# Transposing the convolution's weights among the set-up work, with the matmul fills and the written order renumbered

## The chip, the cores and the metric

The kernel runs on one core of one Trainium2 chip. Its time is the device time of one execution, in microseconds (us); the number given for a kernel is the median of several runs. The profile is of one execution of its own, which has its own time.

Engines are named as in the profile: PE is TensorE (matmuls and transposes), PEld its weight loads, DVE is VectorE, ACT is ScalarE, POOL is GpSimd and SP is SyncE, which here only issues DMAs. Each works through its own queue in order and waits on semaphores for the others.

## What is computed

Linear attention without softmax, a root-mean-square norm over each head, then a feed-forward block with a convolution of three taps along the sequence as its gate. Batch 8, 8 heads, sequence 576, head size 64, model width 512, hidden width 1024:

```python
kv = np.einsum('bhsd,bhse->bhde', k, v)
out = np.einsum('bhsd,bhde->bhse', q, kv)
rms = np.sqrt(np.mean(out * out, axis=-1, keepdims=True) + 1e-06)
x = out / rms * g_norm                      # then heads are joined: [8, 576, 512]
h = np.maximum(x @ w_in, 0.0)
hp = np.concatenate([zeros, h, zeros], axis=1)          # one row on each side
conv_out = sum(conv_w[k][None, None, :] * hp[:, k:k + S, :] for k in range(3))
gate = 1.0 / (1.0 + np.exp(-conv_out))
out = (h * gate) @ w_out
```

conv_w has the shape 3 x 1024: three taps for each hidden channel.

## The kernel before

**Groups.** The 8 batches are worked in five groups: batch 0, batch 1, then 2 and 3, 4 and 5, 6 and 7. For each group the attention is computed with its result transposed (channels on partitions), then `h` in blocks of 128 channels, then the convolution and the gate, then the product with `w_out`, 128 rows at a time, stored to HBM.

**Attention of batch 0.** It comes in two parts, of six and two heads, so that work can begin when six heads have landed. `kv_mm` makes k^T v into `kv_ps`; `kv_out` copies that to `kv_sb`. For each pair of heads `tr_mm` transposes q into `qT_ps`, `tr_out` copies it to `qT`; `out_mm` multiplies qT and kv into `ot_ps`. From `ot_ps`, `square` (on ACT) makes the squares for the norm and `keep` copies the product, scaled by `g_sb`, to `o32`. `ss_mm` sums the squares over each head with the matrix `sel`, `ln_exp` (ACT) makes 1/rms of it, `rb_mm` spreads that over the partitions with the matrix `spread32`, into `rb_ps`, and `x_mul` (DVE) multiplies it to `o32`, which gives `xT`.

**The convolution.** For batch 0 it runs on PE, with diagonal matrices `diag` (one 128 x 128 for each tap and block) as weights, into `c_ps`. The other groups convolve on DVE and ACT: a `tap` is h times a weight for each partition, taken from `cw_rel`, and `add` adds it at its shift. `cw_rel` holds the outer taps divided by the middle one, and the middle one itself, which the sigmoid on ACT applies as its scale.

**The weights of the convolution.** `cw_rows`, 24 x 128 in float32, is loaded by SP as it lies in HBM. A transpose on PE (`cw_mm`) puts the channels on partitions, in `cw_ps`; `cw_out` (DVE) copies it to `cw`. Then `cw_ratio`, eight small DVE operations, makes `cw_rel`, and `cw_diag`, called three times, multiplies the identity by each tap, for `diag`, 128 x 1024 each time.

**Set-up.** Ahead of the groups stand: 14 warm-up matmuls on a tile of ones (`warm`), the loads of k, v and q, the loads of `g_sb` (two, on SP) and of `cw_rows` behind them, the matrix `sel`, 16 transposes of it on PE (`spread_ps`), the copy `spread`, 22 more warm-up matmuls, and `spread32`. This part is put in order by a scheduler from the source; in the built program all 36 warm-up matmuls come first on PE and the 16 transposes behind them.

**The order of the rest.** All that follows is recorded in a plan: each step is an entry with a number, an engine, an estimated cost and what it depends on. The text `ORDER` gives the sequence in which the entries are issued, and so the order in each engine's queue. A letter behind a number picks the engine where there is a choice (a: ACT, d: DVE), and `*n` puts n fills ahead of a PE step: matmuls of `ones` by `ones` into the PSUM buffer that the step then overwrites (`fill`), which compute nothing that is used. An entry on `LAND` issues nothing: it stands for data that have landed at the time given, for whoever makes the order. `Hold` says which steps hold a buffer, for the same purpose.

**Buffers.** PSUM has three buffers of two banks (`ps_two`: `ot_ps`, `rb_ps`, `h_ps`, `c_ps`) and two of one bank (`ps_one`: `warm_ps`, `spread_ps`, `cw_ps`, `kv_ps`, `qT_ps`, `ss_ps`, `o_ps`). Whoever takes a buffer waits until it has been read.

Of the kernel before, what the change touches and what calls it, by code (L numbers as in the profile page):

```python
# [25 lines left out]
def _patch_pnc_remap() -> None:  # L26
# [28 lines left out]
FP32 = mybir.dt.float32  # L55
# [18 lines left out]
PARTS = (3, 1)  # L74
NORM_TABLES = "natural_log_exp_and_others"
ORDER = """
    103 8 11 0 7 17*7 18d 9 19*6 20a 24 21*2 29 25d 26 104 22 30d 27 31*4 32 12 10 34*1 35d 36*1 23a
    37d 33d 41*1 42 38*1 1 43*2 40d 105 13 39 49*2 50 28d 44 2 47*2 106*4 48 6 107a 108 53*2 45*2 54
    3 114*1 109*1 110a 115a 51*1 124 125a 46 119 120a 52 55 64 56a 4 5 65d 111 112 116 117 126 127
    113d 118d 205 212 217 68 128a 121 14 122 66 213d 218a 204 69d 123d 129 130 59 60d 222 82 131 67  # L80
    86 83a 87d 203 70 71 72 57 58 84 85 132 133 223a 134 135 209 210a 138 136 137 208 227 61 139
    228d 62 63 88 89 90 140 141a 148a 235 236d 144 145a 150a 206 146 240 147d 151d 142 143d 149d
    241a 211 214 216a 207 215 367 152 153 154d 157d 155d 156d 158 170 15 164 171a 165a 229 231a 219
    230 232 233a 234 168 169a 73 74d 172d 250 251d 77 78d 75 221a 245 16 159 220 175a 374 79 76 80
    246d 375d 174d 378 379d 81 160 166 167d 242 243 247 249a 248 365 366 94 252 224 173d 244d 176
    177 179d 181d 180d 178d 95a 237 238 225 253 100 101a 226d 382 383d 368 255 256 369 182 96 257 91
    371*1 372d 239a 254a 184 373 258*4 259 185 92a 272*2 273 268*2 269 264*2 265 262*1 263 186 370
    390*1 391a 162 93 260*1 266*1 161 183 386*1 267 270 271 261 97 98a 376 384 377 187 274 393 276
    387a 385 388 389 163 200 394a 288 275d 277d 290d 278 280 279d 289d 281d 201a 392 405 406d 401
    291d 402a 282 523 283a 284 285a 292d 525 532 533d 403 404 524 407 408 397 398d 286 544 545d 380  # L90
    526 527 287a 293d 294 295 296d 299d 298d 297d 300 528 399 400 381 529 530a 531 395 306 320 396
    409 410 411 316 307a 317a 548 549a 202 102 550 321a 412 413 414 415 308 309a 322d 314 315a 324d
    301 318 319d 325d 310 536 311a 551 552d 537d 312 313d 326 559 560a 323d 555*1 556d 327 330d 331d
    328d 329d 538 534 539 332 546 535 540 553 554 541a 561 547 562 194 563 564a 195a 196 99 542 543
    557 558 565 566 188 189a 418 416 567 568 417 336 304 335 424 419 569 425 302 197 303 420 421 190
    422 423 191 192a 193 430 431 428 429 432 433d 444 445a 570 426 427 440 334 305 434 435a 448d
    441a 436 437d 333 337 438 439a 449d 198a 199 446 447a 451d 442 443a 450a 452 453 454d 466 464
    465a 470 467a 471a 457d 455d 359 360a 456a 458 480d 476 477a 478 472 473a 479a 468 571 572 573
    361 469a 481d 483d 474 475a 484 575 482d 485 486d 362 350 462 363a 351a 364 352 459 353 354a 355
    576 577 578 586 579 489a 460 344 345a 461 487d 488d 490 574 590 584 587 591 341 342a 493 347  # L100
    348a 349 346 585 494 492 343 338 580 588 581 582 583 356 589 491 592 593a 598 599a 596 597a 463
    339a 340 600d 622 623a 603d 495 594 595a 604 601a 602d 605 608d 606d 607d 609d 610 646 618 620
    647a 621a 616 617a 624d 627d 619a 628 644 626d 645a 357a 625d 629 631d 630d 632d 613 633d 634
    611 640 358 641a 642 502 643a 614 503a 504 612 648d 650d 649d 615 652 651d 653 654d 656d 655d
    657d 658 520 666 521a 635 522 505 637 506a 507 667a 499 500a 501 517 678 664 638 636 639 665a
    518a 519 668d 669d 687 670 671 659 673d 508 679a 509a 660 672d 510 511 512d 513 661 674 514 662
    702 663 515a 516 680d 676 703a 681 704 682 683d 684 675 677 688a 690 689d 691 692d 696 693 697a
    685 698 699 686 700a 705 701 706d 707 694 695 496 497d 498 708 709a 710 711 717 712a 713 714
    718a 719 715a 716 720 721a 722
"""  # L110
NF = 4
GROUPS = ((0,), (1,), (2, 3), (4, 5), (6, 7))
# [82 lines left out]
def kernel(  # L195
# [11 lines left out]
    nc = tc.nc  # L207
# [3 lines left out]
    P = 128  # L211
# [5 lines left out]
    n_ff = D_ff // P  # L217
# [4 lines left out]
    consts = pool("consts", 1)  # L222
# [8 lines left out]
    ps_one = pool("ps_one", 2, space=PSUM)  # L231
# [8 lines left out]
    def warm(n):  # L240
        for _ in range(n):
            nc.tensor.matmul(warm_ps, ones[:, :P], ones, start=True, stop=True)  # L242
# [34 lines left out]
    def load_w_out(half):  # L277
        fs = slice(half * n_ff // 2, (half + 1) * n_ff // 2)
        nc.gpsimd.dma_start(
            out=w_out_sb[:, fs, :], in_=moe_w_out.rearrange("(f p) m -> p f m", p=P)[:, fs, :])  # L280

    g_sb = consts.tile([P, 1], FP32, name="g_sb")
    for i in range(2):
        nc.sync.dma_start(out=g_sb[i * D:(i + 1) * D, :], in_=g_norm.unsqueeze(1))
    cw_rows = consts.tile([3 * n_ff, P], FP32, name="cw_rows")
    nc.sync.dma_start(out=cw_rows, in_=moe_conv_w.rearrange("k (f p) -> (k f) p", p=P))
    ident32 = consts.tile([3 * n_ff, 3 * n_ff], FP32, name="ident32")
    nc.vector.tensor_copy(ident32, ident[:3 * n_ff, :3 * n_ff])
    eps_sb = consts.tile([P, 1], FP32, name="eps_sb")
# [14 lines left out]
            nc.tensor.transpose(spread_ps[t * SM:(t + 1) * SM, c, :], sel[:, c, :], ident)  # L304
    spread = consts.tile([P, 4, P], BF16, name="spread")
    nc.vector.tensor_copy(spread, spread_ps)
    warm(22)

    spread32 = consts.tile([P, 2, P], FP32, name="spread32")
# [10 lines left out]
    plan = Plan()  # L320
# [3 lines left out]
    def ring(name, bufs):  # L324
        return rings.setdefault(name, Ring(bufs))


    TWO, ONE = ring("two", 3), ring("one", 2)
# [4 lines left out]
    def one_bank(shape, dtype, name):  # L333
        return ps_one.tile(shape, dtype, name=name, tag="one")
# [615 lines left out]
            g.o_ops.append(om)  # L950


    cw = consts.tile([P, 3, n_ff], FP32, name="cw")
    cw_rel = consts.tile([P, 3, n_ff], FP32, name="cw_rel")
    cst = {}

    def cw_mm():
        cst["ps"] = one_bank([P, 3 * n_ff], FP32, "cw_ps")
        nc.tensor.transpose(cst["ps"], cw_rows, ident32)

    def cw_out():
        nc.vector.tensor_copy(cw.rearrange("p k f -> p (k f)"), cst["ps"])

    def cw_diag(j):

        nc.vector.tensor_mul(
            diag[:, j, :, :], ident.unsqueeze(1).to_broadcast([P, n_ff, P]),
            cw[:, j, :].unsqueeze(2).to_broadcast([P, n_ff, P]))
# [10 lines left out]
        for j in (0, 2):  # L979
            nc.vector.tensor_mul(cw_rel[:, j, :], cw[:, j, :], sgn[:, 1, :])  # L980

    landed = plan.op("LAND", 9.0, None)
    mm = plan.op("PE", 0.3, cw_mm, deps=[landed])
    cw_done = plan.op("DVE", 0.2, cw_out, deps=[mm])
    Hold(ONE, mm, [cw_done])
    diag_done = []
    if any(map(any, C_PE)):
        diag = consts.tile([P, 3, n_ff, P], BF16, name="diag")
# [22 lines left out]
    for g in groups:  # L1011
        g.by_act, g.by_dma, g.x_from, g.kv_from = (c[g.n] for c in (BY_ACT, Q_DMA, X_FROM, KV_FROM))
        for b in g.bs:
            for name, src in (("k", k), ("v", v), ("q", q)):
                if b > 0:
                    need = []
                    if b > 1:
# [4 lines left out]
                        deps=[load_ops[name, b - 1]] if b > 1 else [])  # L1022
# [54 lines left out]
```

## Time and profile before

| | |
|---|---|
| median of 4 runs | 200.41 us (200.1 to 200.71) |
| time of the profiled execution | 200.71 us |
| its span, first to last instruction | 198.9 us |
| PE busy | 189.5 us, 95% of the span |
| DVE busy | 153.1 us, 77% |
| ACT busy | 139.0 us, 70% |
| DMA, mean over the span | 158 GB/s |
| diag product on DVE (L966) | 3 of 1.22 us |
| cw transpose on PE (L959) | 1 of 0.24 us, at 16.95 us |
| load of cw_rows (L286), issue | 0.60 us, at 2.00 us |

The time of a run is 1.8 us above the span: what lies around the instructions. The columns of the lines below are, in the chain of waits: start, length, engine, tile, line, how many; in the timeline: start, length, engine, line, operation, what is written and read with sizes, how many, and in brackets the idle time before and what ended it. An "x" after a shape counts instructions. In a list of one line's instructions the three durations are the least, the middle and the most in ns; in the list of waits the three numbers are the time in total, how many waits, and the longest.

How the time passes: up to 8.7 us PE runs warm-up matmuls while k, v and q come in; then batch 0 goes through attention with short steps that hand over between PE, ACT and DVE; from some 30 us on several groups overlap, and near the end there are only products with `w_out` and their stores.

### The profile page before, as it was taken

What the parts mean: (1) busy time and instruction counts of PE and PEld (TensorE: products, weight loads), DVE (VectorE), ACT (ScalarE), POOL (GpSimd) and SP (SyncE); (2) the same over time, 40 slices, a digit from 0 to 9 for tenths busy, and PEclk for the clock granted to TensorE, in tenths of its full rate; (3) what the DMA queues carried; (4) which work ended last, traced back from release to release, by engine and by line L of the source; (5) the groups of instructions that cost most, each with busy time, mean ns of one, the idle gap of its engine ahead of it and who ended that gap; (6) DMA issues with size and microseconds to landing.
All of it is one profiled execution on the core that took longest, in us unless ns stands there. A gap on an engine that the chain in (4) does not pass through costs nothing.

```text
span 198.9 us, 4714 instructions
## 1 busy us (share of the span) xinstructions
PE 189.5 (95%) x1910; PEld 118.5 (60%) x1910; DVE 153.1 (77%) x281; ACT 139.0 (70%) x211; POOL 40.5 (20%) x61
## 2 busy tenths in 40 slices
PE   7999998999999999999999999999999999999990
PEld 4675665887764555777854477654458754644440
DVE  2137678796989876769999999999989999988200
ACT  2036268878869986288897998787988788677131
POOL 7706030012414115011000699110000000000000
PEclk9999999999999999999999999999999999999999
DMA  4999999997899999997779721399551034354653
GB/s 48 199 203 203 205 207 205 203 206 119 124 189 204 226 208 225 203 176 103 182 183 230 228 54 53 94 248 233 146 160 54 0 112 119 86 149 131 164 150 98
DMA packets 32714, 31.49 MB, mean 158 GB/s; under 512 B 2332, under 2 KB 28084, under 8 KB 32692
## 3 DMA queue, kind: packets, MB, share of 16 engines
q0 software_dynamic: 20976, 16.25, 53.5%
q1 hardware_dynamic: 11716, 14.93, 29.0%
q8 instruction: 15, 0.25, 0.5%
q14 instruction: 7, 0.06, 0.1%
HBM read 37.24 MB, written 9.73 MB: 236 GB/s over the span
## 4 chain that ended last, share of the span: by engine, by line
PE 74%; DMA 9%; DVE 8%; ACT 5%; issue 1%; POOL 0%; DVEq 0%; ACTq 0%
PE o_ps L737 27%; PE h_ps L785 24%; DMA v_sb<-in_v_dram 6%; PE warm_ps L242 4%; PE ot_ps L371 3%; DMA kv_sb<-kv_sb 3%; PE qT_ps L460 3%; PE kv_ps L397 2%; PE c_ps L825 2%; PE rb_ps L660 2%; PE o_ps L928 2%; DVE tap L853 2%; ACT qT L349 2%; DVE h L884 2%; DVE conv L875 1%; DVE conv L873 1%
## 5 line engine op out<-in xcount | busy, mean ns | idle before, releaser
L785 PE MATMUL h_ps<-xT,w_in_sb 128*128 128x288 bf16 x512 | 67.4, 286 | 0.4 <-DVE h L798 0.3
L737 PE MATMUL o_ps<-w_out_sb,h 128*128 128x512 bf16 x272 | 61.4, 379 | 0.0
L785 PEld LDWEIGHTS <-w_in_sb 128*128 128x128 bf16 x512 | 48.6, 98 | 15.0 <-issue 2.2
L737 PEld LDWEIGHTS <-h 128*128 128x128 bf16 x272 | 25.7, 98 | 30.6 <-issue 1.4
L879 ACT ACTIVATE conv<-conv,cw_rel 128x576 bf16<-128x576 bf16 (+1 forms) x40 | 37.1, 962 | 1.7 <-DVE conv L875 1.6
L796 ACT ACTIVATE h<-h_ps 128x576 bf16<-128x576 f32 x46 | 28.9, 648 | 8.4 <-PE h_ps L785 8.2
L853 DVE TENSOR_SCALAR tap<-h,cw_rel 128x576 bf16<-128x576 bf16 (+1 forms) x73 | 29.7, 448 | 2.4 <-ACT h L796 1.3
L349 ACT ACTIVATE o_sb<-o_ps 128x512 f32<-128x512 f32 x33 | 19.7, 596 | 15.5 <-PE o_ps L737 10.9
L483 ACT ACTIVATE sq<-ot_ps 128x576 bf16<-128x576 f32 x32 | 19.6, 655 | 4.1 <-PE ot_ps L371 3.7
L884 DVE TENSOR_TENSOR h<-h,conv 128x1152 bf16<-128x1152 bf16 (+3 forms) x16 | 22.0, 1380 | 0.6 <-ACT conv L834 0.5
L864 POOL COPY conv<-h 128x4 bf16<-128x4 bf16 (+3 forms) x12 | 3.9, 324 | 89.4 <-ACT h L796 31.6
L875 DVE TENSOR_TENSOR conv<-conv,tap 128x1152 bf16<-128x1152 bf16 (+11 forms) x36 | 20.4, 621 | 1.1
L873 DVE TENSOR_TENSOR conv<-h,tap 128x1152 bf16<-128x1152 bf16 (+11 forms) x36 | 20.3, 620 | 0.9 <-ACT tap L851 0.4
L349 ACT ACTIVATE qT<-qT_ps 128x576 bf16<-128x576 bf16 x14 | 8.8, 649 | 16.6 <-PE qT_ps L460 16.6
L798 DVE TENSOR_SCALAR h<-h_ps 128x576 bf16<-128x576 f32 x18 | 13.3, 752 | 5.4 <-PE o_ps L928 2.7
L371 PE MATMUL ot_ps<-qT,kv_sb 64*64 64x288 bf16 x192 | 12.2, 297 | 1.9 <-ACT qT L349 0.6
L254 POOL DMA_DIRECT2D q_sb<-in_q_dram x9 | 6.8, 752 | 31.1 <-PE qT_ps L460 26.3
L678 DVE TENSOR_TENSOR xT<-o,rb_ps 128x576 bf16<-128x576 f32 x15 | 10.6, 750 | 3.3 <-PE rb_ps L663 1.6
L684 DVE SCALAR_TENSOR_TENSOR xT<-ot_ps,g_sb,rb 128x576 bf16<-128x576 f32 x16 | 12.2, 810 | 1.1 <-PE ot_ps L371 0.8
L460 PE MATMUL qT_ps<-ident,q_sb 96*128 96x96 bf16 x192 | 12.6, 206 | 0.1
L460 PEld LDWEIGHTS <-q_sb 96*128 96x128 bf16 x192 | 10.5, 97 | 2.5 <-issue 0.8
L371 PEld LDWEIGHTS <-kv_sb 64*64 64x64 bf16 x192 | 5.0, 104 | 9.3 <-issue 7.6
(76 smaller groups left out, 173.9 us busy)
## 6 DMA issues: line engine op xcount, KB each, us to landing
out_dram<-o_sb SPq DMA_DIRECT2D x24, 192.0 KB, 2.3
rb<-scr SPq DMA_DIRECT2D x16, 288.0 KB, 5.7
k_sb<-in_k_dram POOLq DMA_DIRECT2D x7, 576.0 KB, 11.5
v_sb<-in_v_dram POOLq DMA_DIRECT2D x7, 576.0 KB, 13.8
q_sb<-in_q_dram POOLq DMA_DIRECT2D x7, 576.0 KB, 12.0
out_dram<-o_sb SPq DMA_DIRECT2D x24, 128.0 KB, 2.4
out_dram<-o_sb SPq DMA_DIRECT2D x24, 64.0 KB, 2.0
w_in_sb<-in_moe_w_in_dram POOLq DMA_DIRECT2D x2, 512.0 KB, 15.1
```

The costliest lines, as they stand in the source:

```text
L349: nc.scalar.activation(dst, src, AX.Copy, scale=1.0 if scale is None else scale)
L371: nc.tensor.matmul(ps[i * D:(i + 1) * D, e, :HS], kv, g.qT[bi][es, 2 * t + i, :], start=True, stop=True)
L460: nc.tensor.transpose(ps[:, i, j * PS:(j + 1) * PS], q_sb[:, 2 * t + i, j * P:(j + 1) * P], ident[:PS, :PS])
L483: nc.scalar.activation(g.sq[bi, t], ust["ps"][:, :, :HS], AX.Square)
L737: nc.tensor.matmul(st["ps"][:n, :], g.h[:, f, t0:t0 + n], w_out_sb[:, f, :], start=(f == 0), stop=(f == n_ff - 1))
L785: nc.tensor.matmul(ps[:, e, :HS], w_in_sb[:, t, f * P:(f + 1) * P], g.xT[:, t, at:at + HS], start=(t == 0), stop=(t == n_hd - 1))
L796: nc.scalar.activation(dst, st["ps"][:, :, :HS], AX.Relu)
L853: nc.vector.tensor_scalar_mul(dst, src, cw_rel[:, j, f:f + 1])
L873: nc.vector.tensor_add(c[:, :, here], h[:, :, here], t[:, :, there])
L875: nc.vector.tensor_add(c[:, :, there], c[:, :, there], t[:, :, here])
L879: nc.scalar.activation(cst["c"][:, f - f0, :], cst["c"][:, f - f0, :], AX.Sigmoid, scale=cw_rel[:, 1, f:f + 1])
L884: nc.vector.tensor_mul(hs, hs, cst["c"])
```

## The change

Four things are edited.

1. `cw`, `cw_ps`, the transpose and the copy move from the plan into the set-up, behind the copy `spread` and ahead of the 22 later warm-up matmuls in the source. `cw_mm` and `cw_out` are gone as entries of the plan.
2. In their place one entry on `LAND` says that `cw` is there at 6.2 us. Before, an entry said that `cw_rows` is there at 9.0.
3. The load of `cw_rows` is issued on SP ahead of the two of `g_sb`.
4. `ORDER` is a new text. As the plan has two entries fewer, the numbers from 3 on are lower by 2. Once that is taken out, the sequence is the same but for these: `cw_ratio` and the three `cw_diag` stand at its very front (entries 4, 1, 2, 3), where before they stood between the steps of batch 0's norm, and fills are 50 instead of 57.

The fills that are dropped, one at each place, by the new numbers: the first kv product (15, 7 to 6), the third product of batch 0 (29, 4 to 3), an rb (43, 2 to 1; before at 23.53 us), a kv product (369, at 66 us), an rb (262, 2 to 1), a kv product (384, at 70.65 us) and a transpose of q (553, at 100.27 us).

```diff
 ORDER = """
-    103 8 11 0 7 17*7 18d 9 19*6 20a 24 21*2 29 25d 26 104 22 30d 27 31*4 32 12 10 34*1 35d 36*1 23a
-    37d 33d 41*1 42 38*1 1 43*2 40d 105 13 39 49*2 50 28d 44 2 47*2 106*4 48 6 107a 108 53*2 45*2 54
-    3 114*1 109*1 110a 115a 51*1 124 125a 46 119 120a 52 55 64 56a 4 5 65d 111 112 116 117 126 127
...
+    0 4 1 2 3 101 6 9 5 15*6 16d 7 17*6 18a 22 19*2 27 23d 24 102 20 28d 25 29*3 30 10 8 32*1 33d
+    34*1 21a 35d 31d 39*1 40 36*1 41*2 38d 103 11 37 47*2 48 26d 42 45*2 104*4 46 105a 106 51*2 43*1
+    52 112*1 107*1 108a 113a 49*1 122 123a 44 117 118a 50 53 62 54a 63d 109 110 114 115 124 125 111d
...
 """
...
+    cw_rows = consts.tile([3 * n_ff, P], FP32, name="cw_rows")
+    nc.sync.dma_start(out=cw_rows, in_=moe_conv_w.rearrange("k (f p) -> (k f) p", p=P))
     g_sb = consts.tile([P, 1], FP32, name="g_sb")
     for i in range(2):
         nc.sync.dma_start(out=g_sb[i * D:(i + 1) * D, :], in_=g_norm.unsqueeze(1))
-    cw_rows = consts.tile([3 * n_ff, P], FP32, name="cw_rows")
-    nc.sync.dma_start(out=cw_rows, in_=moe_conv_w.rearrange("k (f p) -> (k f) p", p=P))
...
     spread = consts.tile([P, 4, P], BF16, name="spread")
     nc.vector.tensor_copy(spread, spread_ps)
+
+    cw = consts.tile([P, 3, n_ff], FP32, name="cw")
+    cw_rel = consts.tile([P, 3, n_ff], FP32, name="cw_rel")
+    cw_ps = ps_one.tile([P, 3 * n_ff], FP32, name="cw_ps", tag="one")
+    nc.tensor.transpose(cw_ps, cw_rows, ident32)
+    nc.vector.tensor_copy(cw.rearrange("p k f -> p (k f)"), cw_ps)
     warm(22)
...
-    cw = consts.tile([P, 3, n_ff], FP32, name="cw")
-    cw_rel = consts.tile([P, 3, n_ff], FP32, name="cw_rel")
-    cst = {}
-
-    def cw_mm():
-        cst["ps"] = one_bank([P, 3 * n_ff], FP32, "cw_ps")
-        nc.tensor.transpose(cst["ps"], cw_rows, ident32)
-
-    def cw_out():
-        nc.vector.tensor_copy(cw.rearrange("p k f -> p (k f)"), cst["ps"])
...
-    landed = plan.op("LAND", 9.0, None)
-    mm = plan.op("PE", 0.3, cw_mm, deps=[landed])
-    cw_done = plan.op("DVE", 0.2, cw_out, deps=[mm])
-    Hold(ONE, mm, [cw_done])
+    cw_done = plan.op("LAND", 6.2, None)
     diag_done = []
```

## The prediction

> **What bounds the kernel now.** I read first the shares by engine, then the chain of work that ended last, then the timeline of VectorE (DVE) between 9 and 30 us, where the change acts, and last the waits.
>
> ```profile
> PE 189.5 (95%) x1910; PEld 118.5 (60%) x1910; DVE 153.1 (77%) x281; ACT 139.0 (70%) x211; POOL 40.5 (20%) x61
> ```
>
> TensorE (PE) is busy for 189.5 of 198.9 us. Of its 9.4 idle us 1.23 lie before its first matmul and 4.87 after 180 us, so some 3.3 us are spread over everything between: a delay of PE at the start has little to be absorbed in. The chain of waits (start, length, engine, tile, line) around the first attention group:
>
> ```profile
> 8.70 0.34 PE spread_ps L304 x16
> 9.03 0.96 PE kv_ps L359 x7
> 10.00 1.26 PE kv_ps L397 x72
> 11.26 0.84 PE qT_ps L359 x6
> ...
> 12.39 0.66 ACT qT L349
> 13.05 0.04 issue
> 13.09 0.32 PE ot_ps L371 x4
> ...
> 16.42 0.82 DVE o L353
> 17.24 0.04 issue
> 17.28 0.41 PE rb_ps L359 x2
> ```
>
> The reader is to see that the first product of q and kv starts at 13.09, released by ScalarE's (ACT) copy of qT, and that from 17.28 PE runs on almost without a gap. The other operand of that product, kv_sb, is copied by DVE, and it was early:
>
> ```profile
> 9.09 0.42 DVE L306 COPY spread<-spread_ps 128x512 bf16<-128x512 bf16 x1 [4.40 <-PE spread_ps L304]
> 9.55 0.48 DVE L316 SCALAR_TENSOR_TENSOR spread<-spread,neg 128x256 f32<-128x256 bf16 x1
> 11.30 0.56 DVE L351 CAST kv_sb<-kv_ps 128x384 bf16<-128x384 f32 x1 [1.27 <-PE kv_ps L397]
> ...
> 19.63 0.17 DVE L962 COPY cw<-cw_ps 128x24 f32<-128x24 f32 x1
> ...
> 21.77 0.17 DVE L973 TENSOR_SCALAR sgn<-cw 128x8 f32<-128x8 f32 x1
> ...
> 23.02 0.24 DVE L980 TENSOR_TENSOR cw_rel<-cw,sgn 128x8 f32<-128x8 f32 x2
> ...
> 27.19 2.35 DVE L966 TENSOR_TENSOR diag<-ident,cw 128x1024 bf16<-128x1024 bf16 x2
> ```
>
> kv_sb was done at 11.86, so 13.05 - 11.86 = 1.19 us of slack lay between it and the product. The weights' work sat at 19.6 to 29.5, in holes of DVE.
>
> **The change, part by part.** *The place that the weights' work gets.* By the order of the built program, PE still runs all 36 warm-up matmuls (L242) before the 16 spread transposes, although the source has 14 before and 22 behind; the new cw transpose comes after the spread transposes, as row 17, not between the warm-ups. And on DVE the order is: copy of spread, copy of cw, spread32, the eight small operations of cw_ratio, three diag products, and only then the copy of kv_sb. DVE takes its queue in order, so what is added there is ahead of kv_sb.
>
> *DVE, step by step.* The spread copy starts at 9.09 as before and ends at 9.51. The cw transpose (0.24 in its row, L959) runs from about 9.04 to 9.28 and is ready before that. Copy of cw: 0.17 plus a gap of 0.04, 9.72. spread32: 0.48, 10.23. cw_ratio from its first to its last operation took 21.77 to 23.26, 1.49: 11.75. diag: two took 2.35, so a second one starts 1.13 after a first that takes 1.22, and three take 1.22 + 2 x 1.13 = 3.48: 15.25. Copy of kv_sb 0.56: about 15.8 instead of 11.86, 3.9 late. That is 5.2 us of work put into an idle time of 1.27.
>
> *PE until then.* The fill of the first kv now waits for DVE, since cw_ps has taken the buffer of warm_ps and kv_ps must take one that DVE empties: 9.55 (spread copied) to 9.72 (cw copied) instead of 9.03, with six fills for seven (0.96 - 0.84 = 0.12 each). The kv product ends at 11.7 instead of 11.26, still 3.5 before DVE comes to it, so this 0.4 is hidden by the new wait; without that it would be on the path. Then six fills and the first qT transposes, 0.84 + 0.27, to 12.8; ACT copies it to 13.45; the second qT (in the built program it waits for ACT) and two fills, to 14.0; then PE stands until kv_sb at 15.8.
>
> *From kv_sb on.* First product at 15.83 instead of 13.09, 2.74 late: 3.9 less the slack of 1.19. Behind it in PE's queue stand the third qT, the next products and the second part of kv; on ACT the squares, all shifted. The third product was held before by four fills (0.60, to 14.61); now it comes after three, when DVE has copied the third qT. DVE: second qT 15.7 to 16.2 (0.46), third qT 16.55 (its transposes end at 16.35, with drain) to 17.0; product at 17.06. So 17.06 - 14.61 = 2.45 late. What follows is the same row of work to the copy of o (16.42 before) and the first rb at 17.28, which becomes 19.73. The squares on ACT, three of 0.65 from 16.2, end at 18.15, before the copy of o at 18.87, so they don't add.
>
> *What comes back.* From 17.28 to 29.9 the chain holds PE and ACT pieces alone, back to back (rb, ss, kv, qT, h): DVE's xT waits there for rb, not the other way. Taking 5.2 us off DVE there gives the chain nothing; the diag of 27.19 ends at 29.54, 0.1 before h needs DVE. The cw transpose at 16.95 lay beside the copy of o and gives 0; so does the copy of cw. One fill fewer before the rb of 23.53 is on the chain: -0.12. Of four later fills three stand at 66 to 71, before a load that lands at 71.31, the fourth at 100.27 beside ACT's copies; I take 0, bounds -0.5 and 0.
>
> *Queues.* On SP the load of cw_rows goes ahead of the two of g_sb. One issue took 0.60 and g_sb's landing 2.3, so cw_rows lands near 4, wanted at 9.04; g_sb some 0.6 later, wanted after 18. Cost 0; if cw_rows were later than 9.04, all of DVE's sum would move by that. POOL's loads wait for PE's qT, so that of 16.30 moves to about 18.7, those of 27.97 and 41.76 by about 2.3. By 9.34 about 4.0 MB had been issued, 19 us at the 205 GB/s of the slices: the DMA engines have work to about 24, and the next issues are covered alike to 44. Cost 0 there. After that, loads are issued as PE and DVE get on (w_out at 48.84 behind a POOL copy that waits for h), so they keep the distance and so does the delay. Bound: if the landings did not move, PE's waits for DMA there would take up part of it:
>
> ```profile
> PE ot_ps L371 <- DMA kv_sb<-kv_sb: 0.5, 1, 0.5
> PE kv_ps L397 <- DMA v_sb<-in_v_dram: 0.4, 1, 0.4
> ```
>
> 0.9 at most, as PE had no more. I take 0, since what gates these issues is PE's own progress.
>
> *The clock.* PE now stands 0.7 us (12.8 to 13.5) and 1.8 us (14.0 to 15.8), longer than any pause before the tail of this trace. The warm-up shows two speeds of the same matmul (ns least/middle/most), at a granted clock that reads full in both:
>
> ```profile
> L242 PE MATMUL warm_ps<-ones x6: 447/447/448, 4.6 to 5.8; 128*128 128x288 bf16 x6
> L242 PE MATMUL warm_ps<-ones x6: 286/286/286, 7.8 to 8.4; 128*128 128x288 bf16 x6
> ```
>
> Starts are 0.24 apart in the first and 0.12 in the second, and the slow time lasted from 1.23 to about 6.9, 5.6 us. No row shows what a pause of 1.8 does. Bounds: 0, and a slow time as long as the first, 5.6 us at half speed, 2.8 us. I take 0, as the pauses are shorter than that time and broken by matmuls.
>
> The Trainium skill, "TensorE: Matmul & The Clock Gate" (the HAM clock gate), says that PE falls back to half clock after about one idle window, some 3.4 us, and that the window runs free of the kernel. By that rule neither pause is enough and the sum stays as it is; but 12.8 to 15.8 holds only some 0.5 us of matmuls, so it stands closer to that window than a single pause of 1.8 would, and this is the rule that speaks most against the change.
>
> **The sum.** +2.45 - 0.12 = +2.33. Against the profiled execution (span 198.9, its time 200.71): 203.0. That execution is 0.30 above the median of 200.41, so the median should be 200.41 + 2.33 = 202.7.
>
> **Rivals.**
> (a) *The clock falls.* The same delay, and PE at half speed for part of the time from 15.8. For it: 83% of 12.8 to 15.8 idle. Against: no unbroken pause over 1.8. Up to +2.33 + 2.8: 205.5; half of that price gives 204.1.
> (b) *Absorbed later.* The waits for DMA at 58 and 71 take 0.9 and the four fills 0.5: 200.41 + 2.33 - 1.4 = 201.3. Against: these landings follow PE's own issues. If the stage at 17 has slack that I missed too, no change can be told.
> (c) *Faster.* The transposes run between the two warm-ups as the source has them. cw would be in place by about 6, DVE's 5.2 us end by 11.3, and kv_sb is not late. The point is whether cw_ps is ready by 11.30 - 5.2 = 6.1. Then it gains the wait for DVE's h at 30.48 (0.48), eight fills less one that this stage hides (7 x 0.12) and perhaps the 0.24 of the cw transpose: -1.5, 198.9. Against: the built order has all 36 warm-ups first, and spread's transposes ended at 9.04 before too.
>
> **How the numbers follow.** Forecast 0.70 (202.7, its own range 201.8 to 203.7); (a) 0.13; (b) in part 0.07, to no change 0.04; (c) 0.06. A difference within 0.3% (0.6 us) is about what a measurement of this kernel can't tell from none. Slower: 0.70 + 0.13 + 0.07 = 0.90; same 0.04; faster 0.06. The range takes the forecast, the nearer half of (a) and most of (b) in part: 201.4 to 204.8.
>
> **What would show it.** Right: the first copy of kv_sb on DVE at about 15.2, directly behind three diag products; the first ot_ps product at 15.8; the first rb at 19.7; everything from 30 us on later by some 2.3. Wrong: kv_sb copied before 13 (then (c)); warm matmuls' 286 ns gone back to 447 after 16 (then (a)); a delay of 2.3 at 30 us that is under 1 at 75 us (then (b)).

## The result and the profile after

| | before | changed |
|---|---|---|
| median | 200.27 us (17 runs, 200.1 to 202.04) | 202.83 us (12 runs, 201.78 to 207.51) |
| profiled execution | 200.71 | 201.92 |
| its span | 198.9 | 200.1 |
| first copy of kv_sb, end | 11.86 | 14.59 |
| first product of q and kv, start | 13.09 | 14.64 |
| first rb, start | 17.28 | 18.71 |

The ratio is 1.0107, interval 1.0083 to 1.013: slower by about 1%, beyond the 0.3% that can be told from no change. The twelve runs fall apart by the clock that was granted to TensorE (PE), as a mean over the run. Seven had .993 or more and took 201.78 to 202.87, with a median of 202.04. Five had .989 or less and took 202.85 to 207.51. The profiled execution is one of the first kind, so the profile shows the change's cost at full clock and not what the clock added in the others. Medians and ranges here and below are of all runs, while ratios and their intervals leave out runs that lie far above the fastest of the same kernel.

The shares by engine of the changed kernel, to be held against the first line shown of before:

```profile
PE 188.7 (94%) x1903; PEld 117.7 (59%) x1903; DVE 152.9 (76%) x281; ACT 139.0 (69%) x211; POOL 40.5 (20%) x61
```

PE has seven matmuls fewer (the fills) and 0.8 us less work; the other engines do what they did. The time came from waiting, not from work.

The chain of waits of the changed kernel around the first attention group (start, length, engine, tile, line):

```profile
1.23 6.74 PE warm_ps L242 x36
7.97 0.37 PE spread_ps L304 x16
...
8.36 0.42 DVE spread L306
8.78 0.09 DVE cw L312
8.87 0.43 DVE spread L322
...
10.47 0.24 DVE cw_rel L975 x2
10.71 3.41 DVE diag L961 x3
14.12 0.48 DVE kv_sb L357
14.60 0.04 issue
14.64 0.32 PE ot_ps L377 x4
...
17.85 0.82 DVE o L359
18.66 0.04 issue
18.71 0.41 PE rb_ps L365 x2
```

Before, the chain here was PE's and ACT's, and the first product stood behind ACT's copy of qT. Now it runs through VectorE (DVE) from 8.36 to 14.60 without a hole: the copy of spread, cw, spread32, cw_ratio, three diag products, and at last kv_sb, which the product waits for.

The timeline of the changed kernel has the other things to be read (the bracket holds the idle time before and what ended it):

```profile
10.36 1.33 PE L403 MATMUL kv_ps<-v_sb,k_sb 96*64 96x64 bf16 x72 [0.62 <-DMA v_sb<-in_v_dram]
...
13.71 0.41 PE L466 MATMUL qT_ps<-ident,q_sb 96*128 96x96 bf16 x6 [0.74 <-ACT qT L355]
...
14.04 0.55 DVE L357 CAST kv_sb<-kv_ps 128x384 bf16<-128x384 f32 x1
...
14.64 0.32 PE L377 MATMUL ot_ps<-qT,kv_sb 64*64 64x288 bf16 x4 [0.27 <-DVE kv_sb L357]
...
30.98 0.76 DVE L804 TENSOR_SCALAR h<-h_ps 128x576 bf16<-128x576 f32 x1 [2.40 <-PE h_ps L791]
```

The first line was not in the prediction: the first kv product waited 0.62 us for the load of v, which before had come in time. The last line shows what became of the hole that diag left on DVE at 27 us: DVE stands idle there for 2.40 us, waiting for PE. Nothing came back. From 30 us on, everything is about 1.3 us later than in the profile of before (the first `h_ps` 28.98 against 27.67, a wait for v 72.55 against 71.31).

Those 1.3 us are smaller than the change's own cost, because the two executions differ in another thing. The 36 warm-up matmuls took 7.47 us in the profile of before and 6.74 in this one, with the same instructions; in fourteen profiles of this study they took from 6.33 to 7.51. In the changed kernel the start of DVE's row hangs on their end, so the profile after has a head start of 0.73 us. That is also why the signs that the prediction named came early: kv_sb at 14.04 for about 15.2, the first product at 14.64 for 15.8, the first rb at 18.71 for 19.7, and 1.3 us at 30 us for some 2.3. Of the 1.0 to 1.2 us in each, 0.73 is the warm-up.

### The profile page after: what moved, and what is told of

Read it like the earlier page. It is cut to its first block, busy times and chain, and to the rows that moved or that the text cites. A ratio compares the mean times of both kernels' runs of the same rounds, so it can differ in the third digit from the quotient of the medians.

```text
span 200.1 us, 4703 instructions
## 1 busy us (share of the span) xinstructions
PE 188.7 (94%) x1903; PEld 117.7 (59%) x1903; DVE 152.9 (76%) x281; ACT 139.0 (69%) x211; POOL 40.5 (20%) x61
## 4 chain that ended last, share of the span: by engine, by line
PE 71%; DVE 11%; DMA 9%; ACT 5%; issue 1%; POOL 0%; SPq 0%; DVEq 0%; ACTq 0%
PE o_ps L743 27%; PE h_ps L791 24%; DMA v_sb<-in_v_dram 6%; PE warm_ps L242 3%; PE ot_ps L377 3%; DMA kv_sb<-kv_sb 3%; PE qT_ps L466 2%; PE c_ps L831 2%; PE rb_ps L666 2%; PE o_ps L934 2%; DVE tap L859 2%; PE kv_ps L403 2%; DVE diag L961 2%; DVE h L890 1%; DVE conv L881 1%; DVE conv L879 1%
## 5 line engine op out<-in xcount | busy, mean ns | idle before, releaser
L355 ACT ACTIVATE o_sb<-o_ps 128x512 f32<-128x512 f32 x33 | 19.7, 596 | 15.3 <-PE o_ps L743 10.1
```

The lines of the kernel that those rows point to most:

```text
L355: nc.scalar.activation(dst, src, AX.Copy, scale=1.0 if scale is None else scale)
```

## Experiments

Each is the kernel before or the changed one with a small edit. Ratios are to the kernel before, run on the same chip, with the 95% interval. "At full clock" is the median of those runs with a mean granted clock of .99 or more. In the diffs a line of `ORDER` is cut to the stretch that differs.

| run | edit | median (range, runs) | ratio | at full clock | runs below .99 |
|---|---|---|---|---|---|
| changed | | 202.83 (201.78 to 207.51, 12) | 1.0107 [1.0083, 1.013] | 202.0 | 5 |
| e1 | changed, ratio and diag late | 202.99 (201.34 to 206.73, 9) | 1.0084 [1.0045, 1.0123] | 201.4 | 6 |
| e2 | changed, diag late | 204.04 (201.33 to 207.1, 6) | 1.0111 [1.0047, 1.0176] | 201.5 | 4 |
| e3 | changed, 8 fills more in the pause | 202.74 (202.32 to 206.09, 6) | 1.0104 [1.0065, 1.0143] | 202.7 | 2 |
| e4 | before, without the 7 fills | 200.9 (199.3 to 206.13, 12) | 0.9983 [0.9944, 1.0021] | 199.8 | 6 |
| e6 | changed, g_sb loaded first | 212.1 (209.19 to 213.05, 6) | 1.061 [1.0586, 1.0634] | none | 6 |
| e7 | e1, g_sb loaded first | 201.17 (199.6 to 203.66, 12) | 1.0029 [1.0002, 1.0055] | 200.9 | 2 |
| e8 | before, cw_rows loaded first | 201.99 (201.64 to 203.33, 6) | 1.0096 [1.007, 1.0121] | 201.8 | 2 |
| e9 | e2, g_sb loaded first | 200.4 (199.51 to 204.65, 12) | 1.0003 [0.9984, 1.0022] | 200.3 | 3 |
| e10 | e6, 9 fills more in the pause | 202.33 (202.03 to 203.09, 6) | 1.0107 [1.0086, 1.0128] | 202.3 | 0 |
| e11 | changed, with all 57 fills | 202.53 (202.47 to 214.59, 6) | 1.0111 [1.0091, 1.0132] | 202.5 | 3 |
| e12 | e9, with all 57 fills | 201.11 (200.25 to 201.51, 6) | 1.0035 [1.0012, 1.0057] | 201.1 | 0 |
| e13 | before, cw_rows between the two g_sb | 200.92 (200.58 to 201.04, 6) | 1.003 [1.0013, 1.0048] | 200.9 | 0 |

The kernel before had medians of 200.46, 200.42 and 200.15 in the three groups of runs (e1 to e4; e6 to e9; e10 to e13), and 5 of its 54 runs lay below .99.

### The weights' work out of the way of kv_sb: e1 and e2

In e1 the transpose stays early, and cw_ratio and the three diag products go back to where they stood. In e2 only the diag products go back, to the same places as in e1.

```diff
 e1
-    0 4 1 2 3 101 6 9 5 15*6 16d
+    0 101 6 9 5 15*6 16d
...
-    46 105a 106 51*2 43*1 52 112*1
+    46 4 105a 106 51*2 43*1 52 1 112*1
...
-    50 53 62 54a 63d
+    50 53 62 54a 2 3 63d
 e2
-    0 4 1 2 3 101 6 9 5 15*6 16d
+    0 4 101 6 9 5 15*6 16d
```

> The changed kernel, but cw_ratio and the three cw_diag go back to their old places among the steps of batch 0's norm; the early transpose, the DMA order and the fills stay. Theory of the prediction (the DVE queue ahead of kv_sb): kv_sb is copied at 11 to 12 us, the first rb is back at 17.2 to 17.7, the time at 200.0 to 200.7, within 0.3% of before. Rival (the early transpose with its PSUM buffer, or the fewer fills, cost the time): 201.8 or more. Rival (the clock falls because fills are fewer): some runs above 202 with a granted clock under 0.995.

> Only the three cw_diag go back, cw_ratio stays at the front. Theory of the DVE queue: cw_ratio ends at about 11 to 11.7, when the first kv product ends; kv_sb at most 0.5 us late, which is inside the slack of 1.19: 200.0 to 200.7. If each microsecond put ahead of kv_sb cost its share without a threshold: a third of the loss (1.66 of 5.2 us), 200.8 to 201.2.

At full clock e1 took 201.34 to 201.86 and e2 201.33 to 201.6: 0.6 us less than the changed kernel, where the sum of the prediction would have given back all of its 2.3. The timeline of PE in e1 says why:

```profile
10.63 1.33 PE L403 MATMUL kv_ps<-v_sb,k_sb 96*64 96x64 bf16 x72 [1.02 <-DMA v_sb<-in_v_dram]
...
13.98 0.32 PE L377 MATMUL ot_ps<-qT,kv_sb 64*64 64x288 bf16 x4 [0.24 <-ACT qT L355]
...
18.30 0.40 PE L365 MATMUL rb_ps<-ones 128*128 128x288 bf16 x2 [0.32 <-DVE o L359]
```

kv_sb is early again, and the product waits for ACT as before. But v is 1.02 us late, and all behind it with it. So there are two delays, and DVE's queue had hidden the other. That cw_ratio in front (1.49 us on DVE) costs nothing beside e1 agrees with the 1.19 us of slack and the lateness of v. Both kernels also lost clock in most of their runs, 10 of 15 between them, though neither has a pause in front of kv_sb. That their pause for v brought this is not shown: in the profile of e2 the clock is full until 21.9 us, 11 us behind that pause.

### The order of SP's loads: e8, e13

What makes v late? The only edit ahead of it is the load of cw_rows, moved ahead of the two small loads of g_sb. e8 is the kernel before with that swap alone; e13 puts cw_rows between the two.

```diff
 e8
+    cw_rows = consts.tile([3 * n_ff, P], FP32, name="cw_rows")
+    nc.sync.dma_start(out=cw_rows, in_=moe_conv_w.rearrange("k (f p) -> (k f) p", p=P))
     g_sb = consts.tile([P, 1], FP32, name="g_sb")
     for i in range(2):
         nc.sync.dma_start(out=g_sb[i * D:(i + 1) * D, :], in_=g_norm.unsqueeze(1))
-    cw_rows = consts.tile([3 * n_ff, P], FP32, name="cw_rows")
-    nc.sync.dma_start(out=cw_rows, in_=moe_conv_w.rearrange("k (f p) -> (k f) p", p=P))
 e13
-    for i in range(2):
-        nc.sync.dma_start(out=g_sb[i * D:(i + 1) * D, :], in_=g_norm.unsqueeze(1))
+    nc.sync.dma_start(out=g_sb[:D, :], in_=g_norm.unsqueeze(1))
     cw_rows = consts.tile([3 * n_ff, P], FP32, name="cw_rows")
     nc.sync.dma_start(out=cw_rows, in_=moe_conv_w.rearrange("k (f p) -> (k f) p", p=P))
+    nc.sync.dma_start(out=g_sb[D:2 * D, :], in_=g_norm.unsqueeze(1))
```

> The kernel before with nothing but cw_rows ahead of g_sb on SP. Theory A: the DMA rate between 5 and 7 us falls from 190 to 200 GB/s to some 95 to 120, the first v lands at 10.3 to 10.6, the time grows by 0.7 to 1.3: 201.0 to 201.6 in runs at full clock. Rival (the late v of the other runs has another cause, or is hidden): 200.2 as before.

> The kernel before with cw_rows between the two loads of g_sb on SP. If it is the later issue of the last g_sb load (1.9 instead of 1.3 us) that slows k and v: the DMA rate at 5 to 7 us falls to 95 to 130 GB/s, v lands near 10.4 and the time is 201.2 to 202.0 as in e8_swap. If it is cw_rows going ahead of both: the rate stays at 190 to 200, v lands at 9.1 to 9.4, and the time is 200.0 to 200.7.

The swap alone costs 0.96% (1.0096, 1.007 to 1.0121), as much as the whole change. One late load of g_sb costs a third of that, 0.3% (1.003, 1.0013 to 1.0048), which lay between what was expected of either theory. The DMA issues up to 12 us show it, first of before and then of the changed kernel (queue, KB of one, median us from issue to landing):

```profile
v_sb<-in_v_dram POOLq DMA_DIRECT2D x1, 432.0 KB, 6.8
...
g_sb<-in_g_norm_dram SPq DMA_DIRECT2D x2, 0.2 KB, 2.3
```

```profile
v_sb<-in_v_dram POOLq DMA_DIRECT2D x1, 432.0 KB, 8.1
...
g_sb<-in_g_norm_dram SPq DMA_DIRECT2D x2, 0.2 KB, 4.1
```

The loads of g_sb are 256 bytes each, issued 0.5 us later, and the first 432 KB of v come 1.3 us later. The same stretch by windows, for the kernel before, the changed one, e8 and e13 in turn (from:to, length, busy us and instructions of PE, PEld, DVE, ACT and POOL, PE's granted clock, share of the DMA engines, GB/s):

```profile
5.00:7.00 2.00, 2.00 (x11) 1.25 (x9) 0.00 (x0) 0.00 (x0) 2.00 (x4) 1.00 1.30 194
```

```profile
5.00:7.00 2.00, 2.00 (x16) 1.48 (x14) 0.00 (x0) 0.00 (x0) 2.00 (x4) 1.00 0.88 108
```

```profile
5.00:7.00 2.00, 2.00 (x19) 1.57 (x17) 0.00 (x0) 0.00 (x0) 2.00 (x4) 1.00 0.97 132
```

```profile
5.00:7.00 2.00, 2.00 (x15) 1.42 (x13) 0.00 (x0) 0.00 (x0) 2.00 (x4) 1.00 1.17 166
```

194 GB/s before; 108 and 132 with both g_sb behind cw_rows; 166 with one. In the profiles of e4, e6, e7, e9, e10 and e12, all with g_sb in front, it is 193 to 202. So the order of three loads with 12.5 KB between them decides whether 0.17 MB of k and v come in these two microseconds or later (86 GB/s less, for 2 us). Why two loads of 64 times 4 bytes are cheap from 0.7 us on and dear from 1.2 us on, when the loads of k (issued at 1.29) and v (at 2.22) are beginning, these runs don't say; nor do they separate the later g_sb from the earlier cw_rows, as e13, which has one of the two g_sb late, lies in between in time and in rate.

### Giving the old order back to the changed kernel: e6, e10

If late v were a delay of its own, the changed kernel should gain or stay as it is when g_sb goes first again. e6 does that. e10 does it and puts eleven fills in place of two ahead of the first product, where PE waits for kv_sb.

```diff
 e6 and e10
-    cw_rows = consts.tile([3 * n_ff, P], FP32, name="cw_rows")
-    nc.sync.dma_start(out=cw_rows, in_=moe_conv_w.rearrange("k (f p) -> (k f) p", p=P))
     g_sb = consts.tile([P, 1], FP32, name="g_sb")
     for i in range(2):
         nc.sync.dma_start(out=g_sb[i * D:(i + 1) * D, :], in_=g_norm.unsqueeze(1))
+    cw_rows = consts.tile([3 * n_ff, P], FP32, name="cw_rows")
+    nc.sync.dma_start(out=cw_rows, in_=moe_conv_w.rearrange("k (f p) -> (k f) p", p=P))
 e10
-    18a 22 19*2 27 23d
+    18a 22 19*11 27 23d
```

> The changed kernel with g_sb's two loads ahead of cw_rows on SP again; cw_ratio and cw_diag stay at the front. Theory A (two delays beside each other, of which DVE's queue is the longer: v lands about 1.2 us later with the new SP order, kv_sb waits until about 14 for DVE in any case): v lands at 9.1 to 9.4 instead of 10.4, PE then stands longer before kv_sb, the first rb stays at 18.5 to 19.5, the runs at full clock stay at 201.6 to 202.2. Theory B (the late v is the whole loss): 200.2.

> As e6_sp (g_sb ahead of cw_rows, weights' work at the front of DVE), with eleven fills instead of two before the first product of batch 0: 9 x 0.12 = 1.1 us of matmuls in the pause of 1.15 us in which PE waited there for kv_sb. Theory (that pause is what lets the clock fall in every run of e6_sp): granted clock above 0.98 in most runs and times of 201.5 to 203, about 10 us less than e6_sp. Rival (the clock falls from the light matmuls of the rb stage behind it, whatever the pause): 209 to 213 again.

Taking a fault away made the kernel 9 us slower, in all six runs: 212.1. That was beyond what either theory allowed. In e6 the windows show PE's work thin out and then its clock fall:

```profile
13.00:15.00 2.00, 0.66 (x8) 0.35 (x7) 2.00 (x3) 0.39 (x1) 0.00 (x0) 1.00 1.31 207
15.00:17.00 2.00, 1.75 (x24) 0.94 (x24) 1.02 (x3) 1.31 (x3) 0.00 (x0) 1.00 1.32 202
17.00:19.00 2.00, 2.00 (x39) 1.43 (x38) 0.68 (x3) 1.23 (x2) 0.12 (x1) 0.54 1.32 203
19.00:21.00 2.00, 2.00 (x14) 0.66 (x9) 1.59 (x4) 0.94 (x2) 2.00 (x3) 0.60 1.32 205
```

and the timeline where PE stood:

```profile
13.44 0.41 PE L466 MATMUL qT_ps<-ident,q_sb 96*128 96x96 bf16 x6 [0.74 <-ACT qT L355]
13.69 0.41 PE L365 MATMUL ot_ps<-ones 128*128 128x288 bf16 x2
15.26 0.32 PE L377 MATMUL ot_ps<-qT,kv_sb 64*64 64x288 bf16 x4 [1.15 <-DVE kv_sb L357]
```

With v in time, PE does its first kv product sooner and then has longer to wait for DVE: 0.74 and 1.15 us where the changed kernel has 0.74 and 0.27. The clock falls to half soon after. In e10 DVE's queue is the same, and PE works through the pause:

```profile
13.00:15.00 2.00, 1.84 (x22) 1.17 (x19) 2.00 (x4) 0.00 (x0) 0.00 (x0) 1.00 1.32 206
15.00:17.00 2.00, 2.00 (x47) 1.28 (x44) 0.50 (x2) 1.82 (x4) 0.00 (x0) 1.00 1.32 202
```

```profile
14.74 0.32 PE L377 MATMUL ot_ps<-qT,kv_sb 64*64 64x288 bf16 x4 [0.16 <-DVE kv_sb L357]
```

The clock stays at 1.00 and all six runs take 202.03 to 203.09. Two things follow. Some 9.8 us of e6 are the clock's, brought on by the pause. And e10 has DVE's queue with v in time and the clock kept: 1.07% (1.0086 to 1.0128), 2.1 us. The nine new fills are not on the path, as PE still waits 0.16 us for kv_sb behind them. The seven fills that the change drops are missing in e10 too, so its 2.1 us are what the queue costs less what those fills give.

### Fills in the changed kernel's own pause: e3

```diff
-    18a 22 19*2 27 23d
+    18a 22 19*10 27 23d
```

> The changed kernel with ten fills instead of two before the first product of batch 0, so that PE runs 0.96 us longer in the pause before kv_sb comes. If the runs with a granted clock under 0.995 come from that pause: fewer of them, most runs at 201.7 to 202.2, median about 202.0. If the pause has nothing to do with it: as many runs at 202.8 to 204 as the changed kernel had, median 202.6 to 203.0. If the fills overrun the pause: up to 0.9 us more in all runs.

It missed its aim, and the third case came. It was laid out for a pause of 1.8 us; the changed kernel's profile has only 0.27 there, so eight fills ran past kv_sb's coming, and the runs at full clock took 202.32 to 202.77, 0.6 us more than the changed kernel's. Two of six lost clock nevertheless. The profile is of one of these two, and there the clock fell at 74 us, behind another wait for v:

```profile
73.93 1.52 PE L403 MATMUL kv_ps<-v_sb,k_sb 96*64 96x64 bf16 x48 [0.57 <-DMA v_sb<-in_v_dram]
```

So e3 says nothing for or against the first pause as a cause, as e6 and e10 do, but it shows that not all clock was lost at the start.

### Neither delay: e7, e9

e7 is e1, and e9 is e2, with g_sb loaded first (the same edit as in e6).

> As e1_late (cw_ratio and cw_diag at their old places, early transpose, fewer fills) and g_sb's loads ahead of cw_rows on SP again. Theory A: both delays are gone, first product of batch 0 at 12.3 to 13.2, the first rb at 16.7 to 17.4, runs at full clock at 199.3 to 200.4, that is 1.2 to 2 less than e1_late's 201.34. Rival (the early transpose and its PSUM buffer cost what was left in e1_late): no better than 201.3.

> As e7_late_sp, but cw_ratio stays at the front (1.49 us of DVE ahead of kv_sb instead of none). Theory A with the slack of 1.19 before the first product: within 0.3 of e7_late_sp at full clock. If what is put ahead of kv_sb counts without a threshold: 1.5 more than e7_late_sp.

Without either delay the time is back: e9 1.0003 (0.9984 to 1.0022), e7 1.0029 (1.0002 to 1.0055). e9 has 1.49 us of cw_ratio ahead of kv_sb, and kv_sb starts 0.32 us after DVE has fallen idle, so it costs nothing: the slack was read rightly, and the three diag products, 3.4 us, are what goes past it. The cleanest pair is e10 and e9, which differ in the place of the diag products and in nine fills that are off the path: 202.3 and 200.3 at full clock, 2.0 us. e7 should have been within 0.3 of e9 and lies 0.6 above it; four of its ten runs counted at full clock read only .990 or .991, and the other six have a median of 200.3. That e9 equals the kernel before is a balance, as the next section shows: what the early transpose costs and what the dropped fills give are about as large.

### The fills: e4, e11, e12

e4 is the kernel before with the seven fills taken out, e11 the changed kernel with them put back, e12 is e9 with them put back. Three of e4's seven places are shown; the others are edited alike.

```diff
 e4
-    103 8 11 0 7 17*7 18d 9 19*6 20a 24 21*2 29 25d 26 104 22 30d 27 31*4 32
+    103 8 11 0 7 17*6 18d 9 19*6 20a 24 21*2 29 25d 26 104 22 30d 27 31*3 32
...
-    44 2 47*2 106*4 48 6 107a 108 53*2 45*2 54
+    44 2 47*2 106*4 48 6 107a 108 53*2 45*1 54
```

> The kernel before with the seven fills dropped that the change drops, nothing else. Theory of the prediction: one of them on the chain, 0.12 us, so 200.0 to 200.4. Rival (the fills keep the clock up, and the change lost it by dropping them): some runs with a granted clock under 0.995 and a median of 200.8 or more.

> The changed kernel with all 57 fills of before at their places. Theory (the dropped fills are the reason that half of the changed kernel's runs lose clock): fewer runs with a clock under 0.99 than its 5 of 12, full-clock runs at 202.0 to 202.4. Rival (fills don't matter to that): 5 of 12 again, median 202.8 to 203.2.

> What is left of the change that costs nothing by the other runs: the early transpose and cw_ratio at the front, with cw_diag at its old places, g_sb ahead of cw_rows and the 57 fills of before. Theory (nothing in the change can gain, as DVE held nothing up at 20 to 30 us): 200.0 to 200.6, no different from before. Rival (an early cw_ratio frees DVE for xT): 199.0 to 199.7.

At full clock e4 took 199.3 to 200.4, a median of 199.8 where the kernel before had 200.4: the fills were on the path, for about 0.6 us. The two profiles give less, 0.3: e4's span is 1.1 us shorter, of which 0.81 is a shorter warm-up (6.66 for 7.47). But 6 of its 12 runs lost clock, against 3 of 20 of the kernel before beside it, and over all runs nothing is gained (0.9983, 0.9944 to 1.0021). It is undecided whether the fills paid for that clock: over the kernels without DVE's long queue and without late v, 11 of 36 runs lie below .99 with 50 fills (e4, e7, e9), and 5 of 66 with 57 (before, e12, e13), but those runs weren't all on one chip. e11 did not do what was expected of fills that keep the clock: three of its six runs lie below .99, and two of these took 214.17 and 214.59, longer than any of the changed kernel. The other four took 202.47 to 202.55. The profile is of the run with 214.59. Here the second transposes of q wait for kv_sb too, so that one unbroken pause stands where the changed kernel's profile has two short ones:

```profile
14.75 0.42 PE L466 MATMUL qT_ps<-ident,q_sb 96*128 96x96 bf16 x6 [1.82 <-DVE kv_sb L357]
```

The clock falls to half at 16.1 us and stays there until 43.5. That is some 12 us, more than in e6, and here v is late; a late v alone thus doesn't keep the clock.

e12 has nothing of the change left on the path but the place of the transpose, and is slower by 0.35% (1.0012 to 1.0057), 201.11 us where 200.0 to 200.6 was expected. Its profile and that of before have nearly the same warm-up, 7.49 and 7.47:

```profile
9.59 1.02 PE L365 MATMUL kv_ps<-ones 128*128 128x288 bf16 x7 [0.36 <-DVE spread L306]
10.54 1.33 PE L403 MATMUL kv_ps<-v_sb,k_sb 96*64 96x64 bf16 x72
...
17.89 0.40 PE L365 MATMUL rb_ps<-ones 128*128 128x288 bf16 x2 [0.26 <-DVE o L359]
```

cw_ps has taken a PSUM buffer of one bank, so the first fill of kv_ps waits for DVE to copy spread; the first rb comes at 17.89 for 17.28, 0.61 later.

## Why the prediction came out as it did

**DVE's queue ahead of kv_sb (forecast +2.45 us on the path): right in place and kind, and nearly in size.** The chain of the changed kernel is the row of work that was written down, and the first product stands directly behind it. From the spread copy to the end of kv_sb it took 14.59 - 8.36 = 6.23 us, for 6.7 worked out: DVE starts an operation some 0.08 us before the one ahead of it has ended, even across kinds (spread copy 8.36 to 8.78, cw from 8.70; diag to 14.12, kv_sb from 14.04), where the working added gaps of 0.02 to 0.04. Against e4, whose warm-up was as long as the changed kernel's (6.66 and 6.74) and whose fills are the same, the first rb is 18.71 - 16.52 = 2.19 later and the span 200.1 - 197.8 = 2.3 longer. e10, with v in time, gives 2.1 us with the seven fills missing; with the 0.3 to 0.6 us that these are worth (e4) the queue itself comes to an estimated 2.4 to 2.7.

**Nothing comes back at 20 to 30 us: right.** The hole left by diag is idle time of DVE, 2.40 us.

**The fill that waits for the spread copy, priced at 0.4 and hidden: right, and 0.4 was 0.6.** In the changed kernel DVE's queue covers it; in e12, where that cover is gone, 0.61 us show.

**The order on SP, "Cost 0": the step that was wrong.** It asked when each load is wanted and found that both land in time, which they did. It didn't ask what the new order does to the loads beside them. With the swap k and v come up to 1.5 us later (the first k 6.8 for 5.3 us after its issue, the first v 8.1 for 6.8), and in the kernel before the swap alone costs 0.96%. In the changed kernel it adds nothing to the time, because the first kv product, late by it, is still done at 11.69, 2.4 us before DVE comes to kv_sb. So the zero in the sum held, but for a reason that the prediction didn't give. The two delays lie side by side and the longer one counts: DVE's queue alone +2.2 us at full clock (e10, 202.3 against 200.15), the swap alone +1.4 (e8, 201.8 against 200.42), both +1.8 (202.0 against 200.27). The first and the last of these lack the seven fills, the swap alone does not.

**The clock, taken as 0 with bounds 0 and 2.8: undersized.** Five of twelve runs lost some, and the median stands 0.8 above the runs at full clock. Had it been 0, the time would have been 202.0; the forecast of 202.7 met a median that is 0.7 cheaper in the delay and fills and 0.8 dearer in the clock. That 202.7 and 202.83 lie so close is luck: two misses of opposite sign cancel. The direction and the place of the delay are not. The bound of 2.8 was too low as well: e6 shows 9.8 us, since the clock there fell at some 17 us, came back, and fell again from about 24 to 37.7 us (worked out from its windows: .75 from 23 to 25, .50 to 35, .73 from 35 to 40). In the changed kernel's profile the late v puts the first kv product 0.7 us later (10.36, for 9.64 in e10 with the same warm-up) and so fills part of the pause: 0.27 us are left where 1.8 were foreseen. That this is why it mostly escapes e6's loss is likely, not shown, as two runs of e11 lost 12 us with v late. The changed kernel's profile is at full clock, so where its five slow-clocked runs lost it is open; e3 and e9, close kin, lost theirs at 74 and 72 us.

**The fills, -0.12 and for the four later ones 0 with bounds -0.5 and 0:** about -0.6 at full clock (e4), at the edge of what the bounds allow together, -0.62; by the two profiles -0.3. Of the three that were dropped in batch 0, two stand in the chain in front of a step that waits for nothing else (the third product, an rb); at 0.12 each these are 0.24, and where the rest went was not traced.

**The rivals.** Faster (c) fell: the transposes do come behind all 36 warm-ups. Absorbed (b) fell: the delay of 1.3 at 30 us is still 1.2 at 72 us, and no wait for a load swallowed it. Clock (a) is what happened in part of the runs, by less than its price in most and more in one; whether it happened there by the pause that (a) names is open.

The Trainium skill, "TensorE: Matmul & The Clock Gate" (the HAM clock gate), ties the fall of the clock to about one window of some 3.4 us idle. The measurement decides otherwise here: e6 lost clock in every run (.931 to .953), and in its profile the fall comes after two pauses of 0.74 and 1.15 us with 0.7 us of matmuls between them. The length of the window does show, in the times for which the clock stayed down (below).

## What to carry to other kernels

Before work is pulled forward, look at what stands behind its new place in the engine's queue and how much slack that has: here 1.19 us, which 1.49 us of small operations barely used and 3.4 us of diag products overran. A small load has a price for its neighbours and not only a landing time, so where three loads change places at the start, compare GB/s by window before calling it free. And one part of a change can't be priced by undoing it alone when its delay covers another, or shortens a pause that the clock would punish: e6 undid a real fault and lost 9 us.

## What the hardware did that was not expected

The clock is touchier and slower to return than its bounds in the prediction. In e8 PE stood once for 1.63 us, for v:

```profile
9.00:11.00 2.00, 0.42 (x27) 0.42 (x28) 0.00 (x0) 0.00 (x0) 0.58 (x2) 1.00 1.31 201
11.00:13.00 2.00, 2.00 (x62) 1.53 (x56) 0.56 (x1) 0.00 (x0) 0.59 (x1) 0.71 1.31 201
13.00:15.00 2.00, 2.00 (x20) 1.39 (x18) 0.46 (x1) 0.65 (x1) 0.00 (x0) 0.50 1.31 205
15.00:17.00 2.00, 2.00 (x33) 1.09 (x31) 0.46 (x1) 1.47 (x3) 0.00 (x0) 0.93 1.32 201
```

PE was idle for 1.58 of the 2 us from 9 to 11; then the clock was at half for 3.4 us, through matmuls that left no gap. Four of e8's six runs kept a clock of .995 or more; whether they had the same pause no trace shows.

The windows give the times at which the clock changed. In e6, besides those shown above:

```profile
23.00:25.00 2.00, 2.00 (x8) 0.97 (x8) 0.76 (x1) 0.56 (x2) 0.00 (x0) 0.75 1.26 199
...
35.00:40.00 5.00, 4.52 (x43) 2.91 (x41) 1.37 (x2) 2.86 (x6) 2.30 (x3) 0.73 0.85 108
```

A mean of .75 over 2 us is 1.00 us at .50, so the clock fell at 24.0; in the same way .73 over 5 us is 2.7 us at .50, to 37.7. The same working with windows of half a microsecond, on every profile in which the clock fell in the course of the kernel, gives:

| profile | at half clock, us | length, us | in units of 3.41 us | mean clock of the run |
|---|---|---|---|---|
| e8 | 11.85 to 15.26 | 3.41 | 1 | .989 |
| e6 | 17.17 to 20.59, 24.00 to 37.65 | 3.42, 13.65 | 1, 4 | .953 |
| e3 | 74.07 to 80.90 | 6.83 | 2 | .982 |
| e9 | 72.09 to 78.92 | 6.83 | 2 | .982 |
| e2 | 21.89 to 35.54 | 13.65 | 4 | .961 |
| e11 | 16.14 to 43.45 | 27.31 | 8 | .931 |

So in these traces the clock goes by steps of 3.41 us, and the times lost come in steps too. By this table the changed kernel's four runs of .985 to .989, 0.8 to 1.9 us above the median of its others, would be one step each, and its run of 207.51, with .961, four: an estimate from the means alone.

Five of the seven falls come at most 1.9 us after a pause of PE of 0.57 to 1.82 us has ended (e9's was 0.98, for v). The other two, in e2 and the second in e6, have no pause before them: the profile counts PE as busy throughout, but for some 2.3 of the 3.41 us before the fall with the float32 products of `rb_mm`, which have 32 rows. Pauses of up to 1.02 us (e1, for v) also passed without a fall. The profile's busy share therefore doesn't tell when the clock falls, and these runs leave open what does.

The length of the warm-up differs from one execution to the next, 6.33 to 7.51 us for the same 36 matmuls, since the step from the slow matmuls (447 ns) to the fast ones (286 ns) doesn't come at a fixed time: it lies near 7 us in the profile of before and near 5 in e2's. A difference of up to 1.2 us between two profiles near their start can be that alone.

No version beat the kernel before beyond doubt: e9 equals it, and e4 is faster only while the clock holds.
